# Threshold attention and SwiGLU on one core: another cut of the early score bursts and newly written engine orders

## The chip, the cores and the metric

One core of a Trainium2 chip runs the program. The metric is device time in microseconds, the median of several executions; less is better. A profiled execution gives the trace from which the tables below are read.

## The reference

```python
# q, k, v: [8 batches, 8 heads, 576 positions, 64]
scores = (q @ k.T) / 8
thresh = max(scores, axis=-1) - tau                 # tau = 0.02
scores = where(scores >= thresh, scores, -1e9)
attn   = softmax(scores)                            # few entries per row survive
x      = (attn @ v) as [4608 tokens, 512]           # heads side by side
xn     = x / rms(x) * rms_g
out    = (silu(xn @ w_gate) * (xn @ w_val)) @ w_out # d_ff = 1536
```

## The kernel before

**Units.** A *step* is one pair of heads for 128 query rows; a *chunk* is four steps (all eight heads), 36 chunks and 144 steps in all. The 64 rows that are left of each batch's 576 are paired over two batches into chunks of kind "v". For each step TensorE (PE) writes the scores of two heads, 128 x 576 float32 each, into PSUM ("S", a burst; in `emit_burst`). VectorE (DVE) copies them negated by an eighth to one of three score buffers `ssb` and takes the row minimum in the same instruction ("r", `ttr`; where a step is cut in two, the second piece starts from the first one's minimum, `mxp`). GpSimd (POOL) adds tau ("n", `nthr`). ScalarE (ACT) applies a Prelu with a slope of 1e30 for each head ("p") and one Exp for both ("x"), which leaves float16 weights in `wsb`. The weights are transposed, for steps 0 to 15 by PE with two VectorE copies ("T", "S" on VectorE), later by a DMA from SP's queue ("t" on SP). Per two steps an AV unit ("A", `emit_av`) multiplies them with `va`, and VectorE normalizes half a row of `xsb` ("h"). After each chunk ACT or DVE squares and sums ("S" on ACT, `sq`), POOL makes the root and scales ("m", "N"), and the row is transposed to `xnT` (the first four chunks by PE, "x").

The feed-forward part (`emit_ffn`) goes by groups of 2, 2 and then eight times 4 chunks. For each of 12 slices of d_ff: a gate unit "G" and a value unit "V" of four matmuls on PE, a tanh on ACT ("t"), silu and gate products on DVE ("s", "g"). Per chunk of a group two output pieces "O" of six matmuls follow, then an eviction ("e") and a store ("s" on SP). For the last group the O matmuls run slice by slice.

**Inputs.** Batch 0 is loaded in a way of its own, with PE transposes ("t"), batch 1 likewise ("q", "k", "l" on PE, loads "L" on SP); from batch 2 on, blocks are loaded, moved within partitions by POOL copies ("s" on POOL, `swap`) and transposed on DVE ("t", "T", "u"). The gate and value weights come in twelve loads of 0.5 MB on SP's queue ("i") to three staging buffers `stg`, and POOL scales and casts each in two halves ("c", two per load); the first four slices need the first eight casts. The output weights come in four DMAs that POOL issues ("M").

**Bursts.** `CHOP` and `plan_bursts` cut the stream of score columns. A PSUM ring of eight banks of 512 columns is used; kind "w" makes one burst per step, 1024 one burst of 1024 columns for each head (1.78 steps), 1536 one of 2.67 steps. A piece that ends inside a step adds a minimum instruction for each head.

**Order.** The sequence of each engine is written out by hand in `ORDER`: a letter per unit, digits for the PSUM banks, ".n" to take the n-th waiting unit. `in_order` reads it and interleaves the engines so that each unit's producers come first; an engine runs its own list in this order and waits on semaphores for the others. The costs in `COST` and `DMA_NS`, the priorities (`W_FROM`, `B1_BASE`) and the gates (a unit that may come only after a given step's burst; `GATE`, `gated`) describe the units; here they decide nothing but which written orders are accepted, since every emission follows the lists.

In the profile nearly all instructions carry line L98, the recorder `call` of class `Tap`; units are told apart by their tiles.

```python
            t = ttr_of[s, h] = add("DVE", 75.0 + (hi - lo) / 0.96, s - 1 + TTR_EARLY + 0.001 * h, ...)
...
    for o, step in gates:
        if step > 0:
            o.deps.append(s_of[int(step)])
    seq = in_order(ops)
```

Of the kernel before, what the change touches and what calls it, by code (L numbers as in the profile page):

```python
# [14 lines left out]
AX = mybir.AxisListType  # L15

COST = dict(
    s_main=965.0, s_virt=960.0, tr_qk=570.0, tr4=230.0, tr_full=440.0, av_main=300.0, av_virt=370.0, ffn4=215.8, warm=3500.0,
    evac_qk=600.0, evac_qk_act=465.0, evac_half=252.0, evac_kt=330.0, evac_kt_act=252.0, prelu=667.0, exp2=1060.0, exp1=666.0, exp0=590.0,
    mask_d=680.0, mask_g=1810.0, take_g=1420.0, pool_shift=780.0, pool_sq=1280.0, pool_sum=850.0, trw=510.0, evac_w=400.0, evac_wp=900.0, rz=210.0, xmul=341.0, sq=612.0, xn=773.0,  # L20
    pool_tiny=302.0, pool_mean=944.0, pool_dma=880.0, cast_v=620.0, cast_vt=475.0, cast_w=665.0,
    sp=420.0, sp_v=600.0, sp_w=600.0, sp_tr=1300.0, sp_qk=680.0, sp_tl=630.0, sp_qb=600.0, swap=790.0, turn=600.0, turn_t=210.0, turn_q=680.0,
)
DMA_NS = dict(qkb=1750.0, qk=1200.0, tl=600.0, v=870.0, vt=700.0, wt=1700.0, xt=800.0, out=600.0, w=875.0, wo=2000.0)

LETTERS = dict(
    PE={"emit_av/fn": "A", "emit_burst/fn": "S", "emit_ffn/gmm": "G", "emit_ffn/omm": "O", "emit_ffn/vmm": "V",
# [14 lines left out]
)  # L42
ORDER = dict(
    PE=(
        "wt.1:0t3t1t.1:7St6t7St2t5t6ST67t2t5ST65t7Sq67A2T75ST72SA6q72ST65T72SA2T67ST67q25SA6T72ST67x2Sq62A7x5ST75T62ST67A2k5ST67G2V6G7A1V2T65ST67G0V2",
        "G5SV6G7A5V2SG6V2G5V7G6V2Sl67G2V5A6G7SV2G6V5G1O7V6Sx6A0Ox3O6OA7SG6V7G0V3G1V4A6G7V6SG6V7G0V6G3V7G1V2G4V5G6V7SA6G0V3G1V7A4A6SO6A0OSO7OA2SG6A0V7",
        "G3V1G6A2V7SG6V0G3V1G4V6A7A2SG6V7A0O6SG7V0G3A1O.1:7V2SG0V3G1V4G2V5SOA0A3OA5SO6OSG6V0G7V3G1V4G6V2G0V7G5V6SA7A6A0G3V7O6OSG6V0G3A1V4O7A6SG6V0G3",
        "V1A6G4V2A6SOO6OA5SG6V0G3V1G4V6A7SA6G7V0G3V1G4V6A7SG6O7V0OSG6V0O7A3G4A2OSV6G7A0V3G1V6G4V7A2SO6OO7SA6G0V3OG1V4G6V7A2SG6V0A3O7G3V1G4V6A2SOG0V3",
        "O6A7SG7V0G3A7OV1O7SG6V0G3V1A4G6V2A5SOO6OSG6V0G3V1G4V6A2A7SG7V0A3G1V6G4V7A2SO6G0OV5SG6V0A3G1O7A4V6SG6V0G3V1G4V6OSA6O7OA6SO6A0A3OSG7V0G6V3G7V1",
        "G6V4G2V7G5V6SO7G0A3A1A4V2OSG6V0G3O7V1A6SG6V0G3OV1G4V6A2SA6O7OSG6V0G3V1A4G7V6A2SG7V0G3A6O7OSV6G7V0A3G2O1V3G0V6G4OV7G2V0A3G6A7O3V7A6G2OV0O6OO0",  # L50
        "OG3V1G7V4G3V7G2V3G6V2G7V6G5V1O0G3OO7V5G6OO0134V6G2V5OG2OV6G5OOOOV6OOOOOOOOOOOOOOOOO",
    ),
    ACT=(
        "lT.1TT.2TT.1TppTTxTppxppTTxVppxppppxxVppSxppxppxppVxSppppxxpVpxppxpptExtppxSttppxptpxSptpxttppxvtvpptxttppxppxppxppSxppxpptttxptpppxStxtptpp",
        "ttptxppxxtpptxppSxppxppSxppxpppxpxptpxptpxtSppxptppxttpxppSxtppxppppxxtptppxSpxppxtptptxppxppxSpppxpxppxppppxttxSptpttpptxxtppppxxpSptxptpxp",
        "SpxpptxtppptpxxSppxppppxxtSptpptxpxpptxtptppxSpxtppppxpxpxtptppxpSxppptxttpSxppxpppxpxppptxptxSptpxppptpxtptxpxSpptxppxpptpStxpxppxpptxptptp",
        "xSpxppxppppxtxptptppxxptpSxtptpSpxpxpptppxpxpxtptSppxpxpptxtptpxppxppxSppxppxpppSpxpptxpttxtpptxptxpptpppxxpSxtptppSpxxptpptpxtpxSpxpppppxxp",
        "txtpppxtpxStptppxpppxSxpptpxpptpxxttttSSttttttttttttteses",
    ),
    DVE=(  # L60
        "zcR.1RRrrCrrRRrrSRSrrSSrrhSSrrVSSrrhVrrSSSSrrhSSrrSSVrrhSSrrxSSrrhxVrrSSSSrrSShrSSrsvghSSsgrrrsrSsgSrrrrrrshggrrrsgrrrssggrrrrsghrsr.1rsrsgg",
        "grrxTrrehxrrtTethrrrrrrssgsghgsrgru.2u.2rrrsrgrrssggssggusturrrgrhssghrrtrrhrgrTrThrrrrrrrrrheert.1rrrshgrsrghusrurrrrrsggrrssghht.1grrrrsrr",
        "htgTuurrrrsTrgshrgtrrrTrrrrsTrsggsgrrrrrhrhehrrrerrrerrrrrrssrggsrgsstgsggrrrTrhthrrsThueurrrrsghgsTgrrhrrrrrrsrgshrgshgtrrTrrrruehterrurrss",
        "ggsrrgrrhrrrhsrgstgsrrghrrrrrsrguerrtrrrshrgsuherTrtrrrgrsTgrThsrshggrrrrrruerrrthrTsegrusgrhsrgrrrrhrsrgsgsrghrrrrersrgtthTrrrsrhgrsrgTeurr",
        "rrrsrgrsrghshgTrrrrrertuuerrrrsrgsTgtsrhhrurrrrghrssrgsrhgrrrrrrsggertrrrrhssghrtrgrrrrrsurgssgergrrrhrTrruhTtrrrrhherrurrerurstrsTrgrTrsgss",
        "ggsgrrrrrrhhhsggrerrrssgrgrrhrrrrsrsggrsrgherrrrrrehrrrrsrghsrghrsrrrgsrsrghrrerrrrrgrhsgssgsgghsheshggsegsgssegsgsggessesgggssggessggeeE",
    ),
    POOL=(
        "SnnnrrrrnnrnrcncccnmncccncNcncmncNcrnccncMnrrMncrccrccmncMncNnscnsssncMsrmnsNsnsssssnsssnsssnmsNnsssnssnmnnnnrr.2NnnmnNrnmsNnnsssssnrnssssns",
        "ssssnmrnsrNsssnssnsmnsNnsnnnnmr.1nNnnmnNr.1nnrrnssnsrsnssrmsssnsssnr.1NsssnssnmNsnsr.1ssnnsmsnsNnmNnnnnsrrnsssssnnrmNsssnsnssnmsnNrnssssssns",  # L70
        "r.1nmNnsmsNsnnsr.1nnrrnnnnmsNrsnrsnsssmnssNsnssr.1nr.1msssnsnNsssnssssmNnsnnsnnnmnnNsrnnsssnssmsNnrsrnmsssnsNnsnsssrssnsssnsmnssNnnnmnr.1nnn",
        "r.1NrrnmNnnnnmrNrnmNnnnnnmnnnNnmnNnmNmN",
    ),
    SP=(
        "MmMmdOdDdDDAOLDLSLOOLiOiiLiLiLLiioOOo.1oiiAiOililttllttlltltltAtaasstataTttttttTtllttTtlTltltslttltlttttaTttstttAataTtattTTsltltAtllltsltttl",
        "TtlttstaatsTttTtTtaallttlttltsltltstATlltttTtTstatTtasattsatsltltttllTttAlltsTttllttTtstTatttaslttlaatllttTstllAttltTlsttTtttaTsttstttattTst",
        "atTatttTttsTttsttstttttttTtsTsTTsssssss",
    ),
)

# [93 lines left out]
def kernel(  # L174
# [35 lines left out]
    wo = sb("wo", [128, NFC, DM], FP16)  # L210
# [493 lines left out]
    def emit_burst(segs, prio, runs):  # L704
# [10 lines left out]
        for run in runs:  # L715
            def fn(o, run=run):
                for s, lo, hi, at in run:
                    _, whole, quads = info[s]
                    p = steps[s][1]
                    for rows, bb, lhs in quads if no_whole or o.quad else whole:  # L720
                        for h in range(2):
                            hs = HALF[h]
                            nc.tensor.matmul(bank[rows, at[h]:at[h] + hi[h] - lo[h]], lhs(hs), k_of(bb, p, h)[hs, lo[h]:hi[h]],
                                             start=True, stop=True)

            n = sum(hi[0] - lo[0] for _, lo, hi, _ in run)
            met = [b for s, lo, hi, at in run for h in range(2) for b in banks(at[h], hi[h] - lo[h]) if b not in first]
            for b in met:
                first[b] = lead
            lead += 9.0 + per_col * n  # L730
            made.append(add("PE", 9.0 + per_col * n, prio if not made else -600.0, deps + made[-1:], fn, mode=2 if no_whole else 1))
            made[-1].touches = sorted(set(met))
        made[0].claims = sorted((b, 0.0 if TILE else x) for b, x in first.items())
        writers = {}
# [23 lines left out]
        for n_, (s, lo, hi, at) in enumerate(segs):  # L758
            head, tail = lo == 0, hi == S
            if head:  # L760
                buf = s % NSB
                held = ssb_user.get(buf, [])
                ssb_user[buf] = exp_of.setdefault(s, [])
            else:
                held = []
            for h in range(2):
                def ttr(o, s=s, lo=lo, hi=hi, at=at[h], h=h, head=head, tail=tail):
                    m = s % 6
                    nc.vector.tensor_tensor_reduce(
                        out=ssb_of(s)[:, h, lo:hi], in0=bank[:, at:at + hi - lo], in1=zcol.to_broadcast([128, hi - lo]),  # L770
                        scale=-1.0 / 8.0, scalar=3.0e38 if head else mxp[m][:, h:h + 1], op0=ALU.add, op1=ALU.min,
                        accum_out=(mx if tail else mxp)[m][:, h:h + 1])

                before = [] if head else [ttr_of[s, h]]
                need = max(writers[b] for b in banks(at[h], hi - lo))
                t = ttr_of[s, h] = add("DVE", 75.0 + (hi - lo) / 0.96, s - 1 + TTR_EARLY + 0.001 * h, (made if TILE else made[:need + 1]) + [o_c, held] + before, ttr)
                t.long = len(segs) > 1 and sum(hi_ - lo_ for _, lo_, hi_, _ in segs) > LONG
                t.reads = list(banks(at[h], hi - lo))
                t.opens = [b for b, last in last_use.items() if (last[1] == h and n_ == len(segs) - 1 if TILE else last == (n_, h))]
# [433 lines left out]
    n = 0  # L1213
# [79 lines left out]


PACE = 16.0
GATE = 0.0
SQ_DVE = (0,)
OUT_DVE = (1,)
LAGS = ()
CHOP = ((0, 16, 'w'), (16, 24, 1024), (24, 144, 1536))  # L1300
LONG = 1024
TILE = False
TTR_EARLY = 1.0
# [19 lines left out]
PUSH = (40.0, 0.0)  # L1323
EPUSH = (0, 0.0)
V_AFTER = (2, 0, 0, 0)
B1_BASE = 0.0
WO_AT = 0.0
AV_PRIO = 2.5
HALF_PRIO = 1.2
# [14 lines left out]
LAT_QB = 4000.0  # L1344
LAT_V = 3500.0
LAT_W = 2400.0
W_FROM = 2.0
W_STEP = 0.4
N_XPE = 4
SOON = (0, 0.0)  # L1350
N_PE = 16
# [40 lines left out]
```

## Time and profile before

| | us |
|---|---|
| median of 3 runs | 535.59 |
| lowest, highest | 532.46, 536.45 |
| the profiled execution | 533.01 |
| its span, first to last instruction | 531.2 |
| PE busy | 510.2 (96%) |
| VectorE busy | 458.2 (86%) |
| ScalarE busy | 442.4 (83%) |
| GpSimd busy | 223.7 (42%) |

A busy share is of the span; what lies around the span is 1.8 us. The page divides the span into 40 slices of 13.3 us. Since matmuls are pipelined, the busy time of PE holds the draining of each; the time from one start to the next shows what a unit takes when it is fed. The tables by stretch have, behind the stretch's length, the busy time and number of instructions of PE, weight loads, DVE, ACT and POOL, then the granted clock, the busy share of the DMA engines and GB/s.

### The profile page before, as it was taken

What the parts mean: (1) busy time and instruction counts of PE and PEld (TensorE: products, weight loads), DVE (VectorE), ACT (ScalarE), POOL (GpSimd) and SP (SyncE); (2) the same over time, 40 slices, a digit from 0 to 9 for tenths busy, and PEclk for the clock granted to TensorE, in tenths of its full rate; (3) what the DMA queues carried; (4) which work ended last, traced back from release to release, by engine and by line L of the source; (5) the groups of instructions that cost most, each with busy time, mean ns of one, the idle gap of its engine ahead of it and who ended that gap; (6) DMA issues with size and microseconds to landing.
All of it is one profiled execution on the core that took longest, in us unless ns stands there. A gap on an engine that the chain in (4) does not pass through costs nothing.

```text
span 531.2 us, 14520 instructions
## 1 busy us (share of the span) xinstructions
PE 510.2 (96%) x5384; PEld 264.9 (50%) x5384; DVE 458.2 (86%) x1260; ACT 442.4 (83%) x648; POOL 223.7 (42%) x478
## 2 busy tenths in 40 slices
PE   7888999999999999999999999999999999999995
PEld 4556565554544545545454545454454554454442
DVE  4899998998999889999998989999999888864652
ACT  5899899999999987998899889989998889871310
POOL 0367787236841366517653277326651321202000
PEclk9999999999999999999999999999999999999999
DMA  8999999999977999999899999798979769563112
GB/s 180 255 250 260 205 170 227 197 156 213 176 132 142 190 207 167 180 177 195 173 158 196 173 194 181 148 227 185 182 143 155 121 127 156 97 127 83 41 39 80
DMA packets 218887, 88.52 MB, mean 167 GB/s; under 512 B 195264, under 2 KB 204992, under 8 KB 218816
## 3 DMA queue, kind: packets, MB, share of 16 engines
q1 hardware_dynamic: 216016, 85.49, 82.2%
q0 software_dynamic: 1600, 1.57, 2.2%
q8 instruction: 42, 0.69, 0.5%
q10 hardware_dynamic: 1200, 0.52, 0.3%
q14 instruction: 29, 0.24, 0.2%
HBM read 37.75 MB, written 9.44 MB: 89 GB/s over the span
## 4 chain that ended last, share of the span: by engine, by line
PE 56%; DVE 12%; ACT 5%; issue 4%; DMA 2%; POOL 1%; SPq 0%; POOLq 0%; DVEq 0%; ACTq 0%
PE bank L98 56%; DVE ssb L98 5%; ACT ssb L98 3%; DVE sl L98 2%; ACT wsb L98 2%; DVE qkt L98 1%; DMA qkx<-in_k_dram 1%; DVE hf L98 1%; DMA vst<-in_v_dram 1%; DVE stg L98 1%; DVE xsb L98 1%; POOL spare L98 1%; POOL qkx L98 0%; DVE mx L98 0%; DVE osb L98 0%
## 5 line engine op out<-in xcount | busy, mean ns | idle before, releaser
L98 ACT ACTIVATE ssb<-ssb,nth 128x576 f32<-128x576 f32 x288 | 209.4, 766 | 12.5 <-POOL nth L98 12.3
L98 DVE CUSTOM_DVE_ANT_0 ssb<-bank,zcol 128x576 f32<-128x576 f32 (+3 forms) x288 | 185.6, 679 | 20.9 <-PE bank L98 14.8
L98 ACT ACTIVATE wsb<-ssb 128x1152 f16<-128x1152 f32 x144 | 165.4, 1158 | 3.1 <-DMA wt<-wsb 1.3
L98 PE MATMUL bank<-qkt 64*64 64x64 f32 (+8 forms) x2272 | 156.2, 410 | 6.0 <-DVE mx L98 3.5
L98 PE MATMUL bank<-xnT,wg 128*128 128x512 f16 (+1 forms) x480 | 113.3, 359 | 2.1 <-DVE mx L98 1.8
L98 PE MATMUL bank<-xnT,wv 128*128 128x512 f16 (+1 forms) x480 | 113.1, 358 | 1.4 <-DVE xsb L98 0.6
L98 POOL TENSOR_SCALAR nth<-mx 128x2 f32<-128x2 f32 x144 | 30.9, 214 | 188.3 <-DVE mx L98 177.8
L98 ACT ACTIVATE th<-bank 128x512 f32<-128x512 f32 (+1 forms) x120 | 64.8, 546 | 49.2 <-PE bank L98 45.1
L98 PEld LDWEIGHTS bank<-qkt 64*64 64x64 f32 x2272 | 72.0, 133 | 65.8 <-issue 23.4
L98 DVE SCALAR_TENSOR_TENSOR sl<-th,bank 128x512 f32<-128x512 f32 (+1 forms) x120 | 74.3, 627 | 19.2 <-ACT th L98 18.7
L98 PEld LDWEIGHTS <-wv 128*128 128x128 f16 x480 | 44.9, 98 | 51.6 <-DVE mx L98 6.1
L98 PEld LDWEIGHTS <-wg 128*128 128x128 f16 x480 | 42.6, 98 | 55.0 <-issue 7.0
L98 PEld LDWEIGHTS <-wt 128*128 128x128 f16 (+1 forms) x1440 | 50.1, 100 | 18.9 <-DVE mx L98 3.3
L98 PE MATMUL bank<-va,wt 128*128 128x65 f16 (+3 forms) x1440 | 54.1, 196 | 0.5 <-DVE wt L98 0.3
L98 PE MATMUL bank<-wo,hf 128*128 128x512 f16 x216 | 50.9, 379 | 0.5 <-ACT ssb L98 0.5
L98 PE MATMUL bank<-wo,stg 128*128 128x512 f16 x216 | 50.9, 379 | 0.4 <-DVE xsb L98 0.4
L98 DVE STREAM_TRANSPOSE qkt<-qkx 128x128 f32<-128x128 f32 (+2 forms) x72 | 41.7, 588 | 0.0
L98 DVE TENSOR_TENSOR stg<-bank,sl 128x512 f16<-128x512 f32 (+1 forms) x60 | 37.0, 630 | 2.8 <-PE bank L98 2.4
L98 DVE CUSTOM_DVE_ANT_0 ssb<-bank,zcol,mxp 128x384 f32<-128x384 f32 (+4 forms) x68 | 32.9, 513 | 5.1 <-PE bank L98 4.1
L98 DVE TENSOR_TENSOR hf<-bank,sl 128x512 f16<-128x512 f32 (+1 forms) x60 | 36.9, 629 | 0.4
L98 POOL COPY spare<-qkx 32x576 f32<-32x576 f32 x48 | 31.6, 657 | 7.1 <-DMA qkx<-in_k_dram 4.5
L98 DVE TENSOR_TENSOR xsb<-bank,rz 128x256 f32<-128x256 f32 x72 | 30.6, 425 | 4.4
(45 smaller groups left out, 372.7 us busy)
## 6 DMA issues: line engine op xcount, KB each, us to landing
vst<-in_v_dram SPq DMA_DIRECT2D x32, 256.0 KB, 4.3
qkx<-in_k_dram SPq DMA_DIRECT2D x24, 288.0 KB, 3.7
qkx<-in_q_dram SPq DMA_DIRECT2D x24, 288.0 KB, 3.8
out_dram<-osb SPq DMA_DIRECT2D x48, 128.0 KB, 2.6
stg<-in_moe_w_gate_dram SPq DMA_DIRECT2D x6, 512.0 KB, 5.7
stg<-in_moe_w_val_dram SPq DMA_DIRECT2D x6, 512.0 KB, 5.3
wt<-wsb SPq DMA_TRANSPOSE x128, 3.7
out_dram<-osb SPq DMA_DIRECT2D x8, 256.0 KB, 3.2
```

What stands on the lines that cost most here:

```text
L98: made = got(*args, **kw)
```

## The change

The score bursts of steps 8 to 15, one step each before, are cut like those of steps 16 to 23: 1024 columns, 1.78 steps. The five written orders are replaced. The numbers of units are the same, but for 62 bursts instead of 66 and 364 minimum pieces instead of 356. Further, the costs of some units are changed, a burst's cost now adds 52 ns for each run of up to 500 columns and a minimum's cost tells whether it starts or continues a step; G units and the weight loads are no longer gated (`GATE`, `W_FROM`, `W_STEP`), and batch 1's inputs have earlier priorities.

```diff
-    s_main=965.0, s_virt=960.0, ... av_virt=370.0, ...
+    s_main=965.0, s_virt=960.0, ... av_virt=325.0, ...
-DMA_NS = dict(..., w=875.0, wo=2000.0)
+DMA_NS = dict(..., w=925.0, wo=3000.0)
...
 ORDER = dict(
     PE=(
-        "wt.1:0t3t1t.1:7St6t7St2t5t6ST67t2t5ST65t7Sq67A2T75ST72SA6q72ST65T72SA2T67ST67q25SA6T72ST67x2Sq62A7x5ST75T62ST67A2k5ST67G2V6G7A1V2T65ST67G0V2",
+        "wt.1:1t0t3t.1:6St6t7t2St6t5t7ST67t2ST62t7Sq25T67ST72A6SA6q72ST65T72ST67A2T65x7Sq67A5T72Sq67T25T72Sk5x6T72A5ST67A2T65ST72A6G5T72SV6G7V2G6A5S",
...
     DVE=(
-        "zcR.1RRrrCrrRRrrSRSrrSSrrhSSrrVSSrrhVrrSSSSrrhSSrrSSVrrhSSrrxSSrrhxVrrSSSSrrSShrSSrsvghSSsgrrrsrSsgSrrrrrrshggrrrsgrrrssggrrrrsghrsr.1rsrsgg",
+        "zCR.1RcRrrrrRRrrSSRrrSSrrVSSrrSShrrVhrrSSSSrrSSrrSxShrrrrrhrSVSrrrSrrrVSSSrrvrrhrrSSxrrSrrSSShrrrrSSrrhSSrsrgrrrrshsgrrgrrrrhssgrrxgsrrghsgr",
...
     POOL=(
-        "SnnnrrrrnnrnrcncccnmncccncNcncmncNcrnccncMnrrMncrccrccmncMncNnscnsssncMsrmnsNs...
+        "SnnnrrnrrrncnrcnccnmNcccncMncMncnMrmrnNccnccnccc.1nrncrrcnmncscNncsrsMncsnscmc...
...
     SP=(
-        "MmMmdOdDdDDAOLDLSLOOLiOiiLiLiLLiioOOo.1oiiAiOililttllttlltltltAtaasstataTttttt...
+        "MmmMddDdDOOODADLLSLOiiLOiiLALLLioio.1ioOiiOillittlOlttittlltlltttAttTttattsaTt...
...
-            lead += 9.0 + per_col * n
-            made.append(add("PE", 9.0 + per_col * n, prio if not made else -600.0, ...
+            took = per_col * n + (9.0 if n > 500 else 52.0)
+            lead += took
+            made.append(add("PE", took, prio if not made else -600.0, ...
...
-                t = ttr_of[s, h] = add("DVE", 75.0 + (hi - lo) / 0.96, ...
+                t = ttr_of[s, h] = add("DVE", (77.0 if head else 132.0) + (hi - lo) / 0.96, ...
...
-GATE = 0.0
+GATE = 100.0
-CHOP = ((0, 16, 'w'), (16, 24, 1024), (24, 144, 1536))
+CHOP = ((0, 8, 'w'), (8, 24, 1024), (24, 144, 1536))
-B1_BASE = 0.0
+B1_BASE = -12.0
-W_FROM = 2.0
-W_STEP = 0.4
+W_FROM = -20.0
+W_STEP = 0.05
```

## The prediction

> **What bounds the kernel now.** I read the rows by slice first, then the stretch table cut where steps 8, 24, 48 and 80 have had their row minimum taken (33.7, 83.5, 157.3, 260.7 us: ends of the pair of minimum reads that closes the step), then the waits, then each engine's instructions in order of time for the first 60 us.
>
> Clock and slices:
>
> ```profile
> PE   7888999999999999999999999999999999999995
> DVE  4899998998999889999998989999999888864652
> ACT  5899899999999987998899889989998889871310
> PEclk9999999999999999999999999999999999999999
> ```
>
> TensorE is above 90% from the fifth slice on and never has its clock reduced. But VectorE and ScalarE are just as full in the first third. The stretches:
>
> ```profile
> 0.00:33.70 33.70, 26.90 (x329) 16.68 (x329) 23.66 (x71) 25.60 (x42) 9.14 (x26) 1.00 0.92 222
> 33.70:83.50 49.80, 45.89 (x622) 29.55 (x623) 45.36 (x144) 45.84 (x71) 37.86 (x71) 1.00 1.03 227
> 83.50:157.30 73.80, 70.49 (x850) 38.16 (x847) 71.26 (x211) 71.48 (x107) 39.30 (x82) 1.00 0.99 175
> 157.30:260.70 103.40, 102.33 (x1089) 50.80 (x1087) 95.97 (x266) 94.91 (x137) 47.94 (x103) 1.00 0.94 179
> 260.70:531.20 270.50, 264.55 (x2503) 129.70 (x2500) 221.98 (x576) 204.57 (x296) 89.45 (x197) 1.00 0.75 142
> ```
>
> The columns are PE, weight load, DVE, ACT, POOL busy. PE's figure flatters: an instruction counts while its pipeline drains. So I price units by the time from one start to the next where the engine was fed: a gate or value unit of 512 tokens 0.863 us (256 tokens 0.44), an O piece 1.295, an AV unit 0.598, a PE transpose of weights 0.505, a one-step score burst 1.133, a burst of 1024 columns 1.890, one of 1536 columns 2.753. With these PE's whole list is 503.4 us, of which 131.5 end with the burst that holds step 48, and 371.9 lie behind it. That burst's last minimum is read at 157.3, and 373.9 us remain to the end of the span: behind step 48 PE is the bound, with almost nothing lost. Ahead of it PE is fed only 131.5 of some 157 us. There VectorE is the bound: priced the same way (a whole-step minimum 0.678, silu or gate product 0.600, half-row normalization 0.556) it has 23.7 us up to step 8 and 141.3 up to step 48: 117.6 of the 123.6 us between. ScalarE has 115.0 there. In 83.5 to 157.3 VectorE works 71.3 of 73.8 busy.
>
> **So two numbers decide:** the time at which step 48's minimum is read, and what PE work is left then.
>
> **The change part by part.** The new costs and the ungated loads issue nothing by themselves: the kernel takes its sequence from the written orders, and a gate (the burst a load or a G unit is tied to) only limits which orders are legal. What runs differently is the burst cut and the five orders.
>
> (1) *Burst cut, steps 8 to 15.* Eight one-step bursts, 8 x 1.133 = 9.06 us, become 4.5 bursts of 1024, 4.5 x 1.890 = 8.51: PE saves 0.56 us, which is all that PE's total changes (502.9). The row minimum of four steps is now cut in two, for two heads: eight more pieces. From the rows below a 384/192 pair starts 0.475 + 0.334 = 0.81 apart (192 then 384: 0.276 + 0.538 = 0.81), a whole one 0.678: 8 x 0.133 = 1.07 us more on VectorE. It is not hidden: it falls where VectorE is the bound.
>
> ```profile
> L98 DVE CUSTOM_DVE_ANT_0 ssb<-bank,zcol 128x576 f32<-128x576 f32 x220 | 156.8, 751 | 20.0 <-PE bank L98 14.8 <-issue 1.9 <-POOL spare L98 1.6
> L98 DVE CUSTOM_DVE_ANT_0 ssb<-bank,zcol,mxp 128x384 f32<-128x384 f32 x32 | 18.4, 612 | 3.3 <-PE bank L98 2.2 <-issue 0.8
> L98 DVE CUSTOM_DVE_ANT_0 ssb<-bank,zcol,mxp 128x192 f32<-128x192 f32 x30 | 11.6, 405 | 1.9 <-PE bank L98 1.9
> ```
>
> (2) *Order of PE, step 8 to 48.* In the old order 12 gate and 12 value units stand ahead of step 24's burst, in the new 7 and 7, and two bursts fewer. PE's list up to and with that burst is 59.7 us instead of 65.2, VectorE's 66.8 instead of 68.5, ScalarE's the same 72.5. So steps come sooner and feed-forward work later; by step 48 it is caught up in G and V (31 each, both orders), but one AV unit (0.598) and one O piece (1.295) that stood ahead of step 48 now stand behind it: 1.89 us, and with rounding PE has 373.9 left instead of 371.9. As PE is the bound there, that is +2.0 us at the end.
>
> (3) *Order of VectorE, to step 48.* Same sums: 142.2 instead of 141.3, that is +1.07 for the pieces, one normalization fewer (-0.56), and of the block transposes one k, two tails more and one q fewer (+0.63 +0.46 -0.70). With the 6 us of idle VectorE between steps 8 and 48 unchanged: step 48 comes 0.9 later. ScalarE has 142.1 instead of 141.4 and trails VectorE by only three score buffers: I take 1.1. From the other side: VectorE can't gain more than those 6 us.
>
> (4) *The start.* The constant memsets on VectorE (1.80 us at 9.63) go ahead of the first transposes, into a 3.5 us idle. They held step 1's first minimum, which PE had ready at about 11.1, until 11.35: 0.3 us won. PE's longest wait, 1.38 us before the last q transposes at 18.82, is laid to VectorE's copies of weights, but their load was the last of three issues at 13.64 to 15.67 and such loads take 4.0 us: it fits the load better, whose place on SP's queue (18 issues ahead of it) is the same in both orders. So that wait stays, and covers the third q load, issued about 2 us later than before and asked for at 14.5. Against the 0.3: GpSimd's first weight cast moves ahead of step 5's threshold. GpSimd goes in order, so the threshold, step 5's two Prelus and then step 4's Exp on ScalarE wait for that load. It was issued at 20.21 and its cast began at 26.87:
>
> ```profile
> 26.87 0.69 POOL L98 TENSOR_SCALAR wg<-stg,rmsg 128x512 f16<-128x512 f32 x1 [0.87 <-DMA stg<-in_moe_w_gate_dram]
> ```
>
> and the view of transfers has for such loads, issue to landing:
>
> ```profile
> stg<-in_moe_w_gate_dram SPq DMA_DIRECT2D x6, 512.0 KB, 5.7
> ```
>
> One 0.65 us issue fewer stands before it on SP's queue, so issue at 19.5; landing at 25.2 to 26.2, cast done 26 to 27, threshold there instead of 25.09: ScalarE starts step 5 near 26.5 where it started near 25.4. Here a rule of the Trainium skill says otherwise: "DMA: Bandwidth & Descriptors", section "Latency and other measured facts", has about 2 us of fixed cost under load, and its table of bandwidth puts 1 MB at 341 GB/s; an estimate from both is 2 + 1.5 = 3.5 us for these 0.5 MB. Then the weights land at 23.0, nothing waits, the start is worth -0.3 and the sum below 0.3 less. The row says 5.7 (3.8 to 8.2 over the first ten), with the DMA engines 0.92 to 1.03 busy; I follow the row. ScalarE then ends step 5's Exp at 30.0 instead of 28.8; step 8's minimum, which needs that buffer, began at 32.25, so VectorE is not held. The same happens once more: step 8's threshold stands behind a cast whose load can be issued only when the second cast has freed its stage (about 28.2): landing 33.9, threshold near 35.1, ScalarE's step 8 at 35.1 instead of 34.84. The second q load leaves SP at about 8.8, takes 4.0 to 6.5 and is now asked for ahead of step 2 (12.87): 0 to 1 us. With 0.3 won and 0.3 lost the start counts 0, between -0.3 and +3.
>
> (5) *SP and GpSimd later.* The output-weight loads leave GpSimd at steps 9, 10, 11 and 21 instead of 14, 15, 17 and 21, 0.85 us each in front of a threshold, while ScalarE has a step in hand: 0, at worst 0.85 x 3. The last weight casts come at step 23 instead of 20; the third of the gate and value columns they serve is used later too.
>
> (6) *The clock.* A stretch of fewer streamed columns speaks against the change: "TensorE: Matmul & The Clock Gate", section "HAM oscillation — how this bites in real kernels", has the clock halve when PE idles for over about 3.4 us, and the section "Part 4: PE-mode transpose" says that transposes don't count as busy. Between steps 8 and 24 non-transpose work in the new order is 16 x 1.06 + 8 x 0.6 + 14 x 0.44 = 28 us of some 49, 57%. By the rule a thin stretch could go at half speed. But the profile has a thinner one at 1.00: the first eight steps (8 x 1.133 + 2 x 0.6 = 10.3 us of 27), with 1.38 us the longest wait. I take 0.
>
> Sum: start 0, step 48 +1.1, work behind it +2.0 = +3.1 us on the span of 531.2: 534.3. The profiled execution took 533.0, the runs shown have median 535.59 (532.46 to 536.45); 535.6 + 3.1 = 538.7.
>
> **Rivals.**
>
> *A: the waits go (25%).* The start wins 0.3, half of VectorE's 6 us idle between steps 8 and 48 goes (its waits are for PE's banks, which a lighter PE list serves sooner: 14.8 us of such waits over the whole run), and 2 of the 6.5 us lost by PE behind 157 us. With +3.1 that is -2.2: 533.4; with VectorE's idle and 4 of the 6.5 gone it is -7.2, 528.4. For it: ScalarE and VectorE have less PE work in their way up to step 24. Against it: VectorE idles only 2.5 of 73.8 us in the third stretch, so nothing can come from there. This is the rival on the other side: not slower.
>
> *B: thresholds behind weight loads (24%).* All twelve loads take 8.2 us, the longest seen, instead of 5.7: +2.5 us at each of three places (steps 5, 8, 10), which ScalarE can't make up, since it and VectorE are full afterwards: +7.5 on D, 546.2. It decides from about 6.5 us of landing on. GpSimd waits 1.6 us for the first ten loads in the old order, which has the thresholds ahead of the casts.
>
> *C: the clock halves (4%).* Over one 10 us stretch it costs up to 5 us in front of step 48, mostly hidden behind VectorE, over steps 8 to 24 (36 us of PE work at half speed in 49) 23 us: 562.
>
> *D: as summed (47%)*, own range 534 to 543.
>
> From these: faster by over 1% (below 530.2) half of A: 0.12; slower by over 1% (above 541.0) B, C and a few of D: 0.31; within 1%, about what a measurement of this kernel can tell from no change: 0.57. The range goes from the lower half of A to B: 530.5 to 546.
>
> **What would show it.** Eight more partial minimum reads, +1.1 us VectorE busy. Step 8's minimum near 33.7, the threshold of step 5 released by a weight cast. Step 24 earlier than 83.5 by about 1 us, step 48 near 158.4, and PE without loss behind it. Wrong would be: step 48 before 155 (A), a POOL wait for weights of over 2 us (B), a clock row below 9 (C), or new waits of PE behind step 48, which this working takes as unchanged.

## The result and the profile after

| | before | after |
|---|---|---|
| median, measured beside each other (22 runs each), us | 533.27 | 532.49 |
| lowest, highest | 532.46, 536.45 | 531.09, 533.55 |
| the profiled execution, its span | 533.01, 531.2 | 533.18, 531.4 |
| PE, VectorE, ScalarE busy | 510.2, 458.2, 442.4 | 508.1, 459.5, 443.9 |

The ratio is 0.9976, 95% interval 0.9966 to 0.9986: 0.24% faster, within the 1% that the forecast counted as no change, and with the other sign than its point. The profiled execution of after lies 0.7 us above its own median, so spans of single profiles are compared over several runs below. Ratios are always to before on the same chip.

The slices of after: PE is at 90% or more from the seventh slice on, with one exception (before: from the fifth), and no slice has a reduced clock. In none of the 22 executions is the mean granted clock under 0.997.

```profile
PE   7887889999989999999999999999999999989995
PEclk9999999999999999999999999999999999999999
```

The stretch table of after, cut at the same times as that of before (columns: length, PE, weight loads, VectorE, ScalarE, GpSimd, clock, DMA share, GB/s):

```profile
0.00:33.70 33.70, 27.98 (x336) 16.90 (x337) 23.53 (x69) 26.21 (x43) 11.21 (x30) 1.00 0.97 228
33.70:83.50 49.80, 42.67 (x561) 28.66 (x558) 46.76 (x164) 47.17 (x73) 33.10 (x64) 1.00 0.99 223
83.50:157.30 73.80, 70.48 (x860) 39.61 (x860) 70.50 (x209) 67.78 (x102) 42.49 (x87) 1.00 0.92 176
157.30:260.70 103.40, 103.28 (x1114) 52.62 (x1111) 96.09 (x263) 95.95 (x137) 48.92 (x104) 1.00 0.98 181
260.70:531.40 270.70, 263.73 (x2488) 130.22 (x2486) 222.61 (x575) 206.74 (x297) 88.25 (x195) 1.00 0.72 141
```

Row by row against before: in the second stretch PE has 3.2 us less and VectorE and ScalarE have 1.4 and 1.3 more, so the steps do run ahead of the feed-forward work. In the fourth PE is busy 103.28 of 103.40 where it was 102.33: it carries the deferred work and has nothing idle left.

The reads of the row minimum in after (count, total, mean ns): 212 whole ones instead of 220 and more pieces.

```profile
L99 DVE CUSTOM_DVE_ANT_0 ssb<-bank,zcol 128x576 f32<-128x576 f32 x212 | 151.0, 751 | 17.0 <-PE bank L99 12.7 <-ACT ssb L99 1.6 <-ACT xn L99 0.7
L99 DVE CUSTOM_DVE_ANT_0 ssb<-bank,zcol,mxp 128x384 f32<-128x384 f32 x32 | 18.3, 610 | 1.9 <-issue 1.9
L99 DVE CUSTOM_DVE_ANT_0 ssb<-bank,zcol,mxp 128x192 f32<-128x192 f32 x32 | 12.2, 406 | 1.1 <-PE bank L99 0.6 <-POOL xn L99 0.3 <-issue 0.2
```

VectorE's waits for PE's banks ahead of whole reads fall from 14.8 to 12.7 us. GpSimd in order of time (start, length; in brackets the idle time before and its releaser), at step 5 and at step 21:

```profile
23.71 0.69 POOL L99 TENSOR_SCALAR wg<-stg,rmsg 128x512 f16<-128x512 f32 x1 [1.91 <-DMA stg<-in_moe_w_gate_dram]
24.48 0.21 POOL L99 TENSOR_SCALAR nth<-mx 128x2 f32<-128x2 f32 x1
...
70.73 0.62 POOL L99 TENSOR_SCALAR va<-vst 128x512 f16<-128x512 f32 x1 [1.54 <-DMA vst<-in_v_dram]
...
72.02 0.87 POOL L99 DMA_DIRECT2D wo<-in_moe_w_out_dram  x1
72.97 0.22 POOL L99 TENSOR_SCALAR nth<-mx 128x2 f32<-128x2 f32 x1
```

Step 5's threshold does stand behind a weight cast that waits for its load, but the load landed early enough: the threshold starts at 24.48, where step 5's minimum had been read at 24.4. At step 21 the same pattern bites: the minimum was read at 69.0, and the threshold comes 4 us later. A PE wait that before has nowhere comes at the last burst:

```profile
466.47 1.04 PE L99 MATMUL bank<-xnT,wg 128*128 128x512 f16 x4 [1.64 <-DVE mx L99]
```

**Where the time is.** When a step's minimum was read, in the profile of each run that matters below (us; "start" and "steps" say whose orders are used up to step 8 and behind it):

| run | start, steps | 8 | 24 | 48 | 72 | end | 8 to 48 | 48 to 72 | 72 to end |
|---|---|---|---|---|---|---|---|---|---|
| before | old, old | 33.7 | 83.5 | 157.3 | 235.4 | 531.2 | 123.6 | 78.1 | 295.8 |
| old_to_72 | old, old | 34.1 | 83.9 | 157.6 | 236.3 | 532.0 | 123.5 | 78.7 | 295.7 |
| start_new | new, old | 33.3 | 83.3 | 156.6 | 234.5 | 529.9 | 123.3 | 77.9 | 295.4 |
| start_old | old, new | 35.6 | 81.7 | 158.0 | 236.4 | 532.0 | 122.4 | 78.4 | 295.6 |
| after | new, new | 33.8 | 79.9 | 157.2 | 235.9 | 531.4 | 123.4 | 78.7 | 295.5 |
| new_to_72 | new, new | 34.3 | 79.9 | 155.7 | 234.1 | 530.2 | 121.4 | 78.4 | 296.1 |
| tail_banks | new, new | 33.9 | 79.8 | 156.3 | 235.2 | 531.0 | 122.4 | 78.9 | 295.8 |

Each row is one execution. Behind step 72 all are alike. Between 8 and 48 the new orders take 121.4 to 123.4 us, the old ones 123.3 to 123.6. Three more profiles with the old steps (start_engines, start_loads and q_sooner, below) have 123.1 each, one more with the new ones (q_later) 122.8: the means are 122.5 and 123.3, a difference smaller than the spread of the new orders. Between 48 and 72 the means of the same profiles are 78.6 and 78.3. Step 8 comes at 33.3 to 34.3 with the new start and at 33.7 to 35.6 with the old one.

### The profile page after: what moved, and what is told of

The parts are those of the page before. It is cut to its first block, busy times and chain, and to the rows that moved or that the text cites. A ratio compares the mean times of both kernels' runs of the same rounds, so it can differ in the third digit from the quotient of the medians.

```text
span 531.4 us, 14442 instructions
## 1 busy us (share of the span) xinstructions
PE 508.1 (96%) x5344; PEld 268.0 (50%) x5344; DVE 459.5 (86%) x1276; ACT 443.9 (84%) x648; POOL 224.0 (42%) x478
## 4 chain that ended last, share of the span: by engine, by line
PE 66%; DVE 5%; DMA 3%; ACT 2%; issue 2%; POOL 1%; SPq 0%; POOLq 0%; DVEq 0%; ACTq 0%
PE bank L99 66%; DVE ssb L99 3%; DMA wt<-wsb 2%; ACT ssb L99 1%; DVE qkt L99 1%; ACT wsb L99 1%; DMA qkx<-in_k_dram 1%; DVE hf L99 1%; DVE sl L99 1%; ACT th L99 0%; DVE xsb L99 0%; POOL spare L99 0%; POOL qkx L99 0%; DVE stg L99 0%; ACT xn L99 0%
## 5 line engine op out<-in xcount | busy, mean ns | idle before, releaser
L99 DVE CUSTOM_DVE_ANT_0 ssb<-bank,zcol 128x576 f32<-128x576 f32 (+5 forms) x288 | 182.9, 671 | 17.5 <-PE bank L99 12.7
L99 PE MATMUL bank<-qkt 64*64 64x512 f32 (+11 forms) x2232 | 155.6, 410 | 5.4 <-DVE mx L99 3.9
L99 PEld LDWEIGHTS bank<-qkt 64*64 64x64 f32 (+1 forms) x2232 | 73.3, 134 | 63.5 <-issue 23.6
L99 PEld LDWEIGHTS <-wt 128*128 128x128 f16 (+1 forms) x1440 | 51.2, 100 | 19.4 <-issue 2.6
L99 DVE CUSTOM_DVE_ANT_0 ssb<-bank,zcol,mxp 128x384 f32<-128x384 f32 (+7 forms) x76 | 36.2, 508 | 3.2 <-issue 2.1
```

The costliest lines, as they stand in the source:

```text
L99: made = got(*args, **kw)
```

## The experiments

### Which part of the run carries it

Theory E: the gain comes ahead of step 72 (the start or the early order). Rival L: it comes behind, where the orders differ too. Two kernels join the orders at step 72.

```diff
 # new_to_72: before, with after's CHOP and its five lists up to step 72's burst
-CHOP = ((0, 16, 'w'), (16, 24, 1024), (24, 144, 1536))
+CHOP = ((0, 8, 'w'), (8, 24, 1024), (24, 144, 1536))
 # old_to_72: the converse, before's CHOP and lists up to there, after's behind
```

> All five lists of the new order up to step 72, of the old one behind it (new burst cut in steps 8 to 15). Theory L (the gain lies behind step 72, where the new order loses less of PE's time to waits for banks): no faster than the kernel before, 533.3 to 534.5. Theory E (the gain is made early, by the sooner steps and the new cut, and the rest is the same): as fast as the changed kernel, 532.0 to 532.7.

> The old lists and the old burst cut up to step 72, the new order behind it. Theory L: as fast as the changed kernel or faster, 531.3 to 532.6. Theory E: as the kernel before, 533.0 to 533.6. Both halves at 532.8 each: the gain is spread evenly.

Measured: new_to_72 532.37 against 532.77, 0.9985 [0.9968, 1.0002]; old_to_72 533.67, 1.0012 [0.9997, 1.0026]. L falls; E is favoured, though each interval touches 1.

Then the joint moved forward, with the new orders only up to step 24 or 40:

> The new order and cut up to step 24, the old order behind: the same lead of 3.6 us at step 24, but the four gate and value units that the old order has there come at once behind it. If feed-forward units put off early are done later at no cost: as new_to_72, 0.5 to 1.3 us faster than before. If the deferred PE work has to be paid in full, as the prediction had it: no faster than before, 0 to 2 us slower.

> The new order and cut up to step 40, the old order behind. If the gain is made in steps 8 to 40: as new_to_72, 0.5 to 1.3 us faster than before. If it is made in steps 40 to 72, where PE lost less time in spite of more work left: as the kernel before, within 0.4 us.

Measured: 540.53, 1.0146 [1.013, 1.0161], and 534.71, 1.0031 [1.002, 1.0042]. At a joint the old order asks for all G and V (or two O pieces) that the new one has deferred, at once: the cost is that of the joint, not of the new order up to there. (For new_to_40 this is argued from its list, which has two O pieces more ahead of a burst; from step 24 to 48 it took 79.0 us, after 77.2.) The stretch table of new_to_24 shows what it is:

```profile
74.00:79.40 5.40, 2.56 (x33) 1.76 (x31) 3.38 (x10) 5.30 (x10) 4.80 (x10) 1.00 0.99 222
79.40:86.20 6.80, 3.21 (x16) 2.28 (x17) 1.71 (x5) 3.94 (x7) 6.21 (x11) 0.50 1.07 256
```

and PE in order of time, its two waits for VectorE's gate products:

```profile
78.16 0.61 PE L99 MATMUL bank<-xnT,wg 128*128 128x256 f16 x4 [2.25 <-DVE hf L99]
...
82.99 1.03 PE L99 MATMUL bank<-xnT,wg 128*128 128x256 f16 x4 [3.78 <-DVE hf L99]
```

The clock fell at 79.4, behind the first wait (2.25 us) and when the second had hardly begun, and was half for 6.8 us (four matmuls of 256 columns took 1.03 us instead of 0.61); step 24 came at 93.1. This is the rival C of the forecast, seen; the profile of after has nothing of it, and its other executions no sign of it in their clock.

### The start

start_new has after's lists up to step 8 and before's orders and cut behind; start_old is the converse.

```diff
 # start_new, the heads of PE's, VectorE's and SP's lists
-"wt.1:0t3t1t.1:7St6t7St2t5t6ST67t2t5ST65t7Sq67A2T75...
+"wt.1:1t0t3t.1:6St6t7t2St6t5t7ST67t2ST62t7Sq25T67...
-"zcR.1RRrrCrrRRrrSRSrrSSrrhSSrrV...
+"zCR.1RcRrrrrRRrrSSRrrSSrrVSSrrSShrrV...
-"MmMmdOdDdDDAOLDLSLOOLi...
+"MmmMddDdDOOODADLLSLOiiL...
```

> The new lists up to step 8 alone (VectorE's memsets first, casts ahead of thresholds), the old order and old cut behind. The prediction's start term: 0, within 0.4 us of the kernel before. If the whole gain came with the start: 0.8 to 1.3 us faster.

> The old lists up to step 8, the new order and cut behind it: start_new's counterpart. If the start is worth 0.9 us and the rest nothing: 0.9 us slower than the changed kernel, as the kernel before, within 0.4 us of it. If the middle carries the gain: as the changed kernel, 0.8 to 1.3 us faster than before.

Measured: start_new 531.71 against 532.74, 0.9983 [0.9975, 0.9992]; start_old 533.34 against 533.31, 1.0002 [0.9984, 1.0021]. The new start alone gives most of the gain (0.9 of 1.3 us); without it there is none to see, though the interval would still allow 0.9 us.

start_engines takes only PE's, ScalarE's and VectorE's heads of these lists, start_loads only SP's and GpSimd's.

> Before, with the new orders of PE, ScalarE and VectorE up to step 8 and the old ones of SP and GpSimd. If the start's gain is made by the engines' orders (the constant memsets ahead of the first transposes, the copies and transposes of weights moved), this keeps all of it: -0.9 us, ratio 0.998, step 8's minimum read near 33.9. If it is made by the loads and casts, this is level with before, ratio 1.000, step 8 near 34.7.

> The complement: before, with the new orders of SP and GpSimd up to step 8 (loads in another order, one weight cast ahead of step 5's threshold) and the old ones of PE, ScalarE and VectorE. By the engines' theory level or slightly slower (0 to +0.3 us, ratio 1.000 to 1.001); by the loads' theory -0.9 us, ratio 0.998. If neither keeps it, the gain needs both.

Measured: 532.94 against 533.07, 1.0002 [0.999, 1.0015], and 532.29, 0.9988 [0.9973, 1.0002]. The engines' orders alone give nothing, the earlier memsets among them; the loads point to a gain of 0.6 us that the interval doesn't part from nothing. What they change is seen in the last load of batch 0's queries, which PE's three transposes of the forecast's 1.38 us wait need (semaphores name it; the trace has each issue and landing):

| | issue | landing | PE's wait | step 8 |
|---|---|---|---|---|
| before | 14.33 | 18.69 | 1.38 | 33.7 |
| old_to_72 | 13.98 | 19.12 | 1.45 | 34.1 |
| start_old | 14.25 | 19.83 | 2.53 | 35.6 |
| av_o_behind_48 (old start) | 14.72 | 20.41 | 2.80 | 35.4 |
| start_engines | 14.33 | 18.61 | 0.62 | 33.6 |
| start_loads | 13.31 | 16.51 | none | 33.3 |
| start_new | 13.11 | 18.16 | 0.86 | 33.4 |
| after | 13.53 | 17.86 | 0.14 | 33.8 |
| new_to_72 | 13.32 | 17.65 | 0.14 | 34.3 |

Nineteen issues stand ahead of this load in both orders, but in before they take until 14.33 and in after until 13.53. SP's queue in before:

```profile
13.64 2.03 SPq L98 DMA_DIRECT2D qkx<-in_q_dram  x3
```

and in after:

```profile
12.94 1.08 SPq L99 DMA_DIRECT2D qkx<-in_q_dram  x2
```

That the wait of before is the load's, and not that of VectorE's copy of weights after which the profile names it, start_loads shows: with the same orders of PE and VectorE the three transposes start at 17.26 there, ahead of that copy, which starts at 18.24. A wait of 1.4 us is still covered (step 8 at 33.7 and 34.1), one of 2.5 or more is not (35.6 and 35.4).

The list of executions has a second trace of it. One stretch of 3.4 us at half speed (so long are the shortest in the traces) lowers an execution's mean granted clock by 0.003, and so does, at most, the drop behind the last matmuls; 0.996 or less takes both, or two stretches. Before has that in 17 of 134 executions, which took 0.4 to 2.0 us longer than the rest on the means of its five series; nine kernels with the new loads and no such joint as that of new_to_24 (after, new_to_72, tail_banks, thresholds_first, start_new, new_to_40, thr_and_tail, new72_thresholds, start_loads) have it in none of 103. That the late load is the cause in each of the 17 is argued from the profiles of q_later and cut_alone below, which have the clock at half behind the wait for it. It is the smaller part of the gain: 17 of 134 executions, each at most 2.0 us longer, make at most 0.25 us of a mean, and the quickest execution of after is quicker than that of before too (531.09 against 532.46).

Two kernels move only these two loads (unit D), a third does so in the best version below.

```diff
 # q_sooner: before, with them ahead of two vtl loads, a vst load and a k load
-"MmMmdOdDdDDAOLDLSLOOLi...
+"MmMmdOdDdDDDAOLLSLOOLi...
 # q_later: after, with them behind two loads of batch 1
-"MmmMddDdDOOODADLLSLOii...
+"MmmMddDdDOOODALLDSLOii...
 # best_q_sooner: thr_and_tail, with them ahead of two vtl loads and a vst load
-"MmmMddDdDOOODADLLSLOii...
+"MmmMddDdDOODDAOLLSLOii...
```

> Before, with one edit: the last two loads of batch 0's queries, which stand behind two vtl loads, a vst load and a k load on SP's queue (issued at 13.64 and 14.33 us), are issued ahead of these four. If the start's gain is the sooner landing of this load, the second is issued near 11.5, lands near 16, TensorE's wait of 1.4 to 2.8 us before its transposes goes, step 8's minimum is read at 33.9 or sooner, and the ratio is about 0.998. If the load is not the cause, level: 1.000.

> After, with the same two loads moved the other way, behind two loads of batch 1 on SP's queue. By the load's theory they are issued near 14.5 to 15.5 instead of 12.94 and 13.53 and land near 19.5 to 20; TensorE waits 1.5 to 3 us for them, step 8's minimum comes at 34.7 to 35.6 instead of 33.9, and the gain of after is gone: ratio to before 1.000 (0.999 to 1.002). If the load is not the cause it stays at 0.9976.

> The best version so far (after with the thresholds ahead of the casts and the two edits near the end, 0.9944), with the same two loads issued ahead of two vtl loads and a vst load. If only TensorE's wait counts, it is gone already in after, and nothing more comes: 0.9944. If what is left of the wait and its spread from run to run count too, 0.993.

Measured against 533.32: q_later 534.52, 1.0025 [1.0011, 1.0038], the gain gone and more; q_sooner 535.93, 1.0044 [1.0023, 1.0064]; best_q_sooner 532.02, 0.9972 [0.9958, 0.9986]. In q_later the load lands at 19.41 and PE waits for it:

```profile
20.13 0.88 PE L99 MATMUL bank<-id,qkx 128*128 128x128 f32 x3 [2.25 <-DMA qkx<-in_q_dram]
```

and in this execution, as by their clock in 4 others of the 12, the clock falls (the stretch table), so that step 8 comes at 37.1:

```profile
20.10:24.40 4.30, 4.24 (x36) 3.03 (x36) 1.02 (x3) 3.33 (x5) 0.63 (x2) 0.64 1.03 312
```

The seven executions without that have a median of 534.1, still no better than before. So a later landing of this load takes the gain away: that part of the load's theory holds. Its other half, "sooner is better", missed. In q_sooner SP stands in front of the moved load for 3.2 us, until PE has transposed what was in its buffer:

```profile
8.41 6.89 SPq L98 DMA_DIRECT2D qkx<-in_q_dram  x6
15.34 1.28 SPq L98 DMA_DIRECT2D vtl<-in_v_dram  x2
```

Six issues take 6.89 us: the fifth leaves only at 14.40, no sooner than in before. The moved loads do land sooner (the second at 17.36) and PE does not wait for them, but all behind them come 4 us later (vtl at 15.34 instead of 10.89); PE then waits 1.1 us each for a later k and a later q load. In this execution the clock was at half twice, for 3.4 us from 10.8 and from 24.4, and step 8 comes at 38.4. The 12 executions fall into two groups: six of them have such a clock (535.9 to 538.4, and a seventh without it took 537.3), the other five took 533.3 to 534.1, level with before. So most of the loss lies in executions whose clock fell; without that the edit gains nothing. In best_q_sooner the pair waits likewise until 12.45. The new order of after issues them at 12.94, half a us behind that moment, and fills the time before it with three vst issues.

### The deferred work

av_o_behind_48 does the deferral alone, in before: one AV unit and one O piece moved from ahead of step 48's burst to behind it, and the normalization that needs the AV behind its minimum.

```diff
 # PE, around step 48
-...A2SG6V7A0O6SG7V0G3...
+...A2SG6V7SA0O6G7V0G3...
 # DVE
-htgTuurrrrsT...
+tgTuurrhrrsT...
```

> The kernel before, with the one AV unit and the one O piece that the new order defers moved from just ahead of step 48's burst to just behind it (and the normalization behind step 48's minimum). The prediction's term, 1.9 us of PE work left behind step 48 with VectorE as the bound ahead of it and PE behind it: 1 to 2 us slower than before. If PE's waits take up what is deferred: within 0.5 us of the kernel before.

Measured: 535.83 against 533.31, 1.0044 [1.0027, 1.006], +2.3 us. From step 48 to 56 and from 56 to 72, before:

```profile
157.30:181.50 24.20, 23.52 (x259) 11.74 (x257) 21.87 (x66) 23.29 (x34) 5.41 (x16) 1.00 0.90 159
181.50:235.40 53.90, 53.59 (x581) 26.64 (x580) 50.19 (x137) 47.85 (x69) 28.24 (x58) 1.00 0.95 183
```

av_o_behind_48:

```profile
158.60:185.10 26.50, 25.82 (x273) 12.92 (x270) 22.58 (x66) 23.40 (x34) 5.43 (x16) 1.00 0.91 145
185.10:239.20 54.10, 53.80 (x581) 26.48 (x580) 50.32 (x138) 47.93 (x69) 28.35 (x58) 1.00 0.94 182
```

after:

```profile
157.20:182.50 25.30, 25.18 (x273) 12.93 (x270) 21.90 (x64) 24.21 (x36) 7.43 (x20) 1.00 0.94 162
182.50:235.90 53.40, 53.40 (x582) 27.14 (x581) 51.04 (x138) 48.18 (x69) 26.48 (x55) 1.00 0.99 187
```

The same 273 matmuls follow step 48 in both. In the old order PE keeps 0.68 us idle in that stretch, and the stretch is 2.3 us longer; in the new one PE's idle falls to 0.12 and none is left to step 72, so it is 1.1 us longer to step 56, of which 0.5 has come back by step 72. Six of the 12 executions of av_o_behind_48 have a mean clock of 0.996 or less; the other six have a median of 535.6, so the loss is not the clock's.

### The burst cut alone

cut_alone is before's order with the new cut; the bursts of steps 8 to 15 are placed where the first score of each stood.

```diff
-CHOP = ((0, 16, 'w'), (16, 24, 1024), (24, 144, 1536))
+CHOP = ((0, 8, 'w'), (8, 16, 1024), (16, 24, 1024), (24, 144, 1536))
 # PE: three S less among steps 8 to 15; DVE: eight more r
```

> The old orders, with steps 8 to 15 cut into bursts of 1024 columns (the last of 512) put where the old bursts stood, and the second pieces of the cut minima right behind their first ones. By the prediction's own term (eight pieces more on VectorE, 1.07 us, where it is full): 0.5 to 1.2 us slower than before. If the cut itself brings the gain (PE -0.5 us, fewer waits of bursts for minima): 0.5 to 1.5 us faster.

Measured: 539.66 against 532.74, 1.0121 [1.0105, 1.0136]. In its profile PE waits 1.2 to 1.9 us three times for the first pieces of minima, the bursts being where the old order had no room for them, and the start had a 2.47 us wait for the query load with the clock at half from 21.1 to 24.5. Three of the four executions have such a clock; the fourth took 538.4, so most of the loss is there without it. The run shows that the cut needs its own order, not what the cut is worth in it. The old cut in the new order was not run.

### Places where after still loses

tail_banks gives the late units other banks and puts one minimum sooner, against the new 1.64 us wait.

```diff
 # PE, DVE
-SOG1A2V6G0V3G2V1G0A6...   rrrrr.2r.2grhrsseg...
+SOG2V6A1G0V3G1V2G0A6...   rrrrr.2r.2grrhsseg...
```

> The changed kernel, with the three G and V units behind the last burst on other PSUM banks and in another order, and step 142's last minimum ahead of a normalization. If the 1.64 us wait of PE at 466.5 us is on the path that sets the end: 1.2 to 1.8 us faster than the changed kernel, 530.7 to 531.3. If PE has slack behind it, or the wait only moves to the next bank: as the changed kernel, 532.0 to 532.7.

Measured: 531.75 against 532.77, 0.9981 [0.9968, 0.9994], not told from after. The wait at 466 is gone, and 1.66 us come at 477 instead, for a gate product (hf).

thresholds_first puts the thresholds of steps 21 to 23 ahead of what GpSimd waits for:

```diff
 # POOL
-...ncsrsMncsnscmcssncNss...
+...ncsnrsMncssncmcsscNss...
```

> The changed kernel, with the thresholds of steps 21, 22 and 23 on GpSimd ahead of the weight casts, the value round and the DMA issue that stand in front of them. If these late thresholds (4.2 us at step 21) hold back the steps behind them: step 24 some 2 us sooner and 0.5 to 2 us faster than the changed kernel, 530.5 to 532. If PE's list decides by the time the delay could reach the end: the same within 0.4 us, 532.1 to 532.9.

Measured: 531.35 against 532.77, 0.9967 [0.9954, 0.998]; step 24 comes at 78.9 instead of 79.9, but the interval overlaps that of after. Two kernels build on it: thr_and_tail has both edits above, and one normalization later near the end (DVE `shsggshgg` to `ssgghshgg`); new72_thresholds is new_to_72 with the thresholds.

> thresholds_first with tail_banks, and one normalization near the end moved behind the silu and gate products that the moved wait (1.66 us at 477 us in tail_banks) stood behind. If PE has no slack there: 1 to 1.7 us faster than thresholds_first, 2.6 to 3.4 us faster than before. If the last group has another bound: as thresholds_first, 1.2 to 2.2 us faster than before.

> new_to_72 with the thresholds of steps 21 to 23 ahead of casts: the new order where it is sooner, the old one where it has no wait at the last burst. If thresholds and tail are two costs of the new order that add up: 1.8 to 2.8 us faster than before. If they don't add: as thresholds_first, 1.2 to 1.8 us.

Measured: thr_and_tail 530.95 against 533.31, 0.9944 [0.9926, 0.9962], the best of all and clear of after, with no PE wait over 1 us near the end and 294.5 us behind step 72; new72_thresholds 532.6, 0.9983 [0.9967, 0.9999], a miss: level with new_to_72, no gain from the thresholds. Its profiled execution, the longest of its 12, reads step 8 at 35.5 (the last section says why).

## Why the prediction was wrong

Point and result lie 6.2 us apart: 2.3 of these are the base (533.27 in 22 runs beside after, 535.59 in the three shown), 3.1 the sum of the change that didn't come, 0.8 the gain that did. The larger miss is the 3.1 of (1) to (3), which came out as nothing that can be told from 0; that left the sign to the start, which was put at 0 and gained.

**Burst cut (1)**: right as a count. 16 new pieces for eight whole reads, VectorE's busy time +1.3 (forecast +1.07); PE's list is 0.56 shorter by its own count, which no run parts out.

**Start (4)**: here the sign was lost. The step that failed is "whose place on SP's queue (18 issues ahead of it) is the same in both orders. So that wait stays". The reading behind it was right: the wait named after VectorE's copies is the load's, and the profiles of six runs name the load outright (waits of 0.62 to 2.80 us). But a place in a queue was counted in issues and not in time. The issues ahead end 0.8 us sooner, and the wait falls from 1.4 (0.6 to 2.8 in the other profiles) to under 0.9; step 8 comes at 34.0 on the mean of the ten profiles with the new loads (33.3 to 35.5), at 34.8 in the six with the old ones (33.6 to 36.6). The 0.3 us from the memsets didn't show (start_engines 1.0002), nor the 0.3 lost at step 5's threshold: the load left at 19.22 and took 4.4 us. For this load the estimate of 3.5 us from the Trainium skill's page "DMA: Bandwidth & Descriptors" (section "Latency and other measured facts", and its table of bandwidth, which was measured with loads issued from GpSimd) was nearer than the row chosen (5.7, median). For such loads in general the row was nearer; after's medians are

```profile
stg<-in_moe_w_gate_dram SPq DMA_DIRECT2D x6, 512.0 KB, 4.9
stg<-in_moe_w_val_dram SPq DMA_DIRECT2D x6, 512.0 KB, 5.2
```

with single landings of 3.9 to 9.6 us. A median over twelve loads at different stages says little about one of them, and "nothing waits" is what came.

**Order to step 48 (2, 3)**: that step 24 comes sooner was right, that step 48 comes later was not. "With the 6 us of idle VectorE between steps 8 and 48 unchanged" failed: summed gaps of VectorE between 33.7 and 157 us are 7.0 in before, 6.3 in after, 4.5 in new_to_72. Step 24 came 3.5 us sooner, not 1: PE's list up to it is 5.5 us shorter, and VectorE, which I had called the bound there, had waited 2.7 us for PE's banks between 33.7 and 83.5 in before; in after it does not wait for them there at all. From 8 to 48 the new order is 0.8 us shorter on the mean (122.5 against 123.3) instead of 1.1 longer.

**Work behind step 48 (2)**: "As PE is the bound there, that is +2.0 us at the end" was right for a deferral by itself (av_o_behind_48, +2.3), and the new order's own stretch costs 0.2 (48 to 72 on the mean, 78.6 against 78.3). The step that failed is the tacit term: that PE's small losses behind 48 are the same in both orders. The working contradicts itself there: it has PE behind step 48 "with almost nothing lost", while rival A takes 2 us out of 6.5 that PE loses. PE's time from 160 to 460 us, beyond its units at their usual time from start to start, is 7.9 us in before and 5.0 in after. Two of these three us lie behind step 72, and most of that is given back at the end, where the new 1.64 us wait is: 295.5 us against 295.8 in all. This is half of rival A, which I had at 25% with VectorE's and PE's idle as its source; start_old (1.0002, -0.9 to +1.1 us) says that (1) to (3), and all else behind step 8, sum to nothing measurable instead of +3.1.

**SP and GpSimd later (5)**: the "0, at worst" for the output-weight loads was right but for step 21: its threshold came 4 us late. Rival B's mechanism (thresholds behind waits for loads) is real at that place; thresholds_first puts its price at about 0.5 us, not told from 0, where B had 7.5, and new72_thresholds didn't repeat even that.

**Clock (6)**: no halving in after, as taken. The rule of the Trainium skill's page "TensorE: Matmul & The Clock Gate", section "HAM oscillation — how this bites in real kernels", puts its limit at idle times of about 3.4 us. Here single waits of 2.25 us (q_later, and the first one of new_to_24) and 2.47 (cut_alone) were followed by half the clock, while 2.53 (start_old) and 2.80 (av_o_behind_48) were not. The traces show why length alone doesn't decide: every recorded stretch of one clock but the last is a multiple of 3.41 us long, on a grid that starts at another moment in each execution. The wait of q_later lies with 1.9 us in one such window:

```profile
16.36:19.77 3.41, 1.43 (x25) 0.69 (x16) 2.89 (x8) 1.65 (x3) 1.76 (x5) 1.00 0.78 138
19.77:23.18 3.41, 3.05 (x15) 2.08 (x17) 0.00 (x0) 2.14 (x4) 0.96 (x2) 0.50 1.05 289
```

That of start_old, from 17.44 to 19.97, is cut in two by the border at 18.71:

```profile
15.30:18.71 3.41, 1.84 (x26) 1.02 (x25) 3.29 (x11) 2.65 (x4) 2.45 (x6) 1.00 0.73 163
18.71:22.12 3.41, 2.15 (x28) 1.70 (x29) 0.67 (x3) 1.54 (x2) 0.00 (x0) 1.00 0.71 161
```

Over all profiles, the last 10 us of each left out, five windows at full clock with 1.9 to 2.4 us of PE idle were followed by half the clock, one with 2.0 was not, and none with less than 1.7. So the measured limit is near 2 us of idle in one window, and whether a wait of 2 to 4 us meets it is in part luck.

**What stays open.** That the loads' order makes the start's gain is favoured by start_loads and by the table of landings, and q_later shows that a late landing undoes it; that this one load is all of it is not shown, since moving it alone forward blocked the queue. How the gain divides between a shorter wait in most executions and the clock kept in the rest is known only roughly, and the cut's share within the new order is open too.

## What to carry to other kernels

A load's place in a queue is a time: add up the durations and buffer waits of the issues ahead of it, and set its landing, with its spread over executions, against the moment when it is asked for. Moved ahead of the moment when its buffer comes free, a load isn't issued sooner and makes every load behind it late. Read the mean clock of the single executions beside the median: a wait that halves the clock in some of them can cost more than its own length, and the profiled execution may be one of these or not. Work deferred past a point costs its full length only if the engine's idle behind that point stays what it was, so an order searched anew has to be priced with the idle that it removes, not with that of the old one.

## What the runs showed of the hardware

PE's transposes at the start take 421 ns and from some moment on 272. That moment is the beginning of the trace's first record of the clock: ahead of the first transpose (4.3 to 4.6 us) in five profiles, by 6.6 us in the others, but at 10.28 in new72_thresholds, where step 8 is 1.6 us late. The rows give 1.00 for the time before that record because they have no record to count; where the clock is recorded as half (q_sooner, at 12.1 us) the same transposes take 421 ns too. So the moment of full clock at the start varies by up to 6 us from execution to execution, and the time of step 8 in a single profile carries that with it. The same load of queries took 2.6 to 5.7 us from issue to landing, by execution and by what was in flight beside it.
